# Waiting on PE instead of SP for the last store of a two-branch decode attention

## The chip, the cores and the metric

The kernel runs on one core of one Trainium2 chip. A core has five engines with an instruction stream of their own: PE (TensorE, the matrix multiplier), DVE (VectorE), ACT (ScalarE), POOL (GpSimd) and SP (SyncE, which here only issues transfers). They meet through semaphores alone. The metric is the device time of one execution in microseconds (us). Three runs of the kernel before gave 246.31, 246.37 and 246.56 us; their median, 246.37 us, is the time before.

## The reference

Two independent decode attentions, A and B, are computed for one token each and their results laid side by side. Both have a row x of 576 numbers, 32 query heads on 16 key and value heads, heads of 128, and caches of 8192 positions; all is bf16.

```
def _B_ref(x, k_cache, v_cache, wq, wo):
    q = (x @ wq).reshape(B, Sq, Hq, Dh).transpose(0, 2, 1, 3)
    k = jnp.repeat(k_cache, rep, axis=1)          # rep = 2
    v = jnp.repeat(v_cache, rep, axis=1)
    scores = jnp.einsum("bhqd,bhkd->bhqk", q, k) * (Dh ** -0.5)
    p = _softmax(scores, axis=-1)
    o = jnp.einsum("bhqk,bhkd->bhqd", p, v)
    return o.transpose(0, 2, 1, 3).reshape(B, Sq, Hq * Dh) @ wo
```

A is the same on the last W = 2048 positions of its caches. The result is [1, 1, 1152]: 576 numbers of A, then 576 of B.

## The kernel before

The kernel is a list of operations for each engine, written by hand: `op(eng, fn, deps, name)` appends an operation to one engine's list, `load(...)` appends one that increments a semaphore of its own when it is done (a transfer counts 16). When all is listed, `emit` walks each list in order and writes the engine's instructions. In front of an operation it writes a wait (line 83, `eng.wait_ge(s, v)`) for each semaphore value that the operation needs and that this engine has not yet waited for. An operation whose function is `None` is its waits and nothing else. Every wait made by the kernel therefore stands under line 83 in the profile, unless it was joined to the instruction behind it. Nothing reorders the lists.

The work runs in this order. SP issues all large loads into one ring in SBUF: the query weights of A and B, then the keys and values of eight units (four of A, four of B, each of four key heads), then the output weights. The output weights of A are one load; those of B come in five pieces of 17, 8, 4, 2 and 1 blocks (`NWO`), so that little work is left when the last piece has landed. PE makes the queries (line 310). For each unit DVE transposes the keys in slabs (line 350), PE makes the scores (line 367), a softmax without its division follows on DVE, PE and ACT, DVE transposes the probabilities (lines 414 and 418) and PE multiplies with the values (line 431). The sums of the exponentials are divided out at the end (lines 488 to 499).

The last stage is the output projection (line 510): for each of A and B, 64 matmuls with one column of weights each into two rows of one PSUM bank. When a branch's last matmul is done, ACT copies 320 of its numbers and DVE the other 256 to the row `outsb` (lines 519 and 521), each adds 1 to that branch's semaphore `s_row`, and SP issues the store of 1152 bytes (line 523), which adds 16 to `s_out` when it has landed. The store of A is named `out0` and that of B `out1`; `out1` stands for `s_out` at 32, which both stores make up. The last operation of the kernel is a wait for `out1` with no function.

POOL writes constants at the start and has nothing to do after that. ACT and DVE have nothing behind their copies of B's output, PE nothing behind its last matmul of line 510.

Of the kernel before, what the change touches and what calls it, by code (L numbers as in the profile page):

```python
# [36 lines left out]
class Prog:  # L37
# [9 lines left out]
    def op(self, eng, fn, deps=(), name=None):  # L47
        self.ops[eng].append((fn, tuple(deps), name, None))
        if name is not None:
            assert name not in self.where, name  # L50
            self.where[name] = (eng, len(self.ops[eng]) - 1)
# [46 lines left out]
def bass_concat_heads__sliding_block_cached__gqa_block_cached__decode_kernel(nc, A_x, A_k_cache, A_v_cache, A_wq, A_wo,  # L98
# [59 lines left out]
    op, load = pg.op, pg.load  # L158
# [74 lines left out]
    def slab(kind, i, s):  # L233
# [10 lines left out]
       deps=["id0"], name="ident")  # L244
# [15 lines left out]
    for c in range(2):  # L260
        op("dve", lambda e, c=c: e.tensor_reduce(par[:, c:c + 1], view(identf, 128, c, [[2, 64]]), AX.X, ALU.add),
           deps=["identf"], name="par%d" % c)
# [3 lines left out]
    for P in range(2):  # L266
# [14 lines left out]
        for c in range(2):  # L281
            op("dve", lambda e, P=P, c=c: e.tensor_scalar(
                xrep[:, P, 4 + c, :], banks[2 * P + 1][:, 0:128], par[:, c:c + 1], None, ALU.mult),
                deps=["xT%d.4" % P, "par%d" % c], name="xr%d.%d" % (P, 1 + c))
# [3 lines left out]
       deps=["identf"], name="clsb")  # L288
    op("dve", lambda e: e.tensor_reduce(clsa[:], view(identf, 128, 0, [[1, 8], [8, 16]]), AX.X, ALU.add),
       deps=["identf"], name="clsa")  # L290
    op("dve", lambda e: e.tensor_reduce(sel[:], view(identf, 128, 0, [[1, 32], [32, 4]]), AX.X, ALU.add),
       deps=["identf"], name="sel")
# [6 lines left out]
    for P in range(2):  # L299
        for n in range(8):  # L300
# [3 lines left out]
            def mm(e, P=P, n=n, bank=bank):  # L304
# [10 lines left out]
               deps=["qmm%d.%d" % (P, n)] + (["qT%d" % (u // 2 - 2)] if u >= 4 else []), name="qe%d" % u)  # L315
            if n % 2:
# [3 lines left out]
                    deps=["qe%d" % (u - 1), "qe%d" % u] + (["z0.%d" % i for i in range(4)] if P else []),  # L320
                    name="qT%d" % (u // 2))
        for b in range(4):
            if P == 1:
# [3 lines left out]
                    deps=["qT%d" % u for u in range(4, 8)] + ["zb0"], name="z1.%d" % b)  # L327
            else:
# [3 lines left out]
                    deps=["qT%d" % u for u in range(4)] + ["za0"], name="z0.%d" % b)  # L332
# [122 lines left out]
    for i in range(NU):  # L455
# [34 lines left out]
       deps=["lsel", "lselA", "nb%d" % last, "mr%d" % last], name="L")  # L490
# [3 lines left out]
        deps=["rl", "O%d" % last], name="on")  # L494
    op("dve", lambda e: e.transpose(oq[:].rearrange("p c k -> p (c k)"), on[:].rearrange("p c k -> p (c k)")),
       deps=["on"], name="oq")
# [6 lines left out]
    for P in range(2):  # L503
        k0 = 0
        for c, kk in enumerate(NWO[P]):
            def mm(e, P=P, c=c, k0=k0, kk=kk):
# [15 lines left out]
             s_row[P], 2, deps=[done], step=1)  # L522
        load("sp", lambda e, lo=lo: e.dma_start(out[0, 0:1, lo:lo + DM], outsb[0:1, lo:lo + DM]),
             s_out, 16 * (P + 1), deps=["f%d" % P], name="out%d" % P)
    op("sp", None, deps=["out1"])

    pg.emit()

# [27 lines left out]
```

## Time and profile before

| what | value |
|---|---|
| median of three runs | 246.37 us (246.31 to 246.56) |
| the profiled execution's own time | 246.6 us |
| its span, first to last instruction | 245.2 us |
| busy: PE, DVE, ACT, POOL | 172.3, 129.1, 24.3, 8.2 us |
| moved by the transfers | 102.90 MB, mean 420 GB/s |
| the last copies of the output row, on ACT and DVE, start | 243.65 us |
| each of these two copies takes | 0.43 us |
| issue of the last store, until SP's last wait is over | 244.1 to 245.2 us |

The page of the profile gives for each engine its busy time and share of the span, a picture of the span in 40 slices, the transfer queues, the chain of work that ended last, and the costliest groups of instructions. The timeline, the chain and the waits come from the same trace. Times count from the span's start. An engine's name with a q behind it (SPq, PEldq) is its sequencer, which waits and issues; such instructions are not counted as busy. The span ends with the last instruction of the program; the profiled execution's own time is 1.4 us longer.

### The profile page before, as it was taken

The page shows a single profiled execution, that of the slowest core. Times are in us where ns is not written, and L with a number is a line of the kernel's source. Part 1 is how long each engine was busy: PE and PEld are TensorE (multiplying, and loading weights), DVE is VectorE, ACT ScalarE, POOL GpSimd, SP SyncE. Part 2 cuts the span into 40 slices and gives each one's busy share as a digit, 9 for nine tenths or more (in the row PEclk, how much of TensorE's full clock was granted, in tenths as well). Part 3 has the DMA queues.
Part 4 walks back from the last instruction along what each step waited for, and adds up shares of the span by engine and source line. Part 5 has one row for each costly group of instructions (what it writes and reads, how often), then busy time and mean ns, then how long its engine had stood idle before and what let it go on. Part 6 is the DMA issues. An engine that isn't in the chain of part 4 may idle for free.

```text
span 245.2 us, 2253 instructions
## 1 busy us (share of the span) xinstructions
PE 172.3 (70%) x960; PEld 71.8 (29%) x961; DVE 129.1 (53%) x162; ACT 24.3 (10%) x52; POOL 8.2 (3%) x15
## 2 busy tenths in 40 slices
PE   0269967787867994889582869945579939257197
PEld 0124422224433222432130523211423213213154
DVE  0422547667789986699501699810679920500201
ACT  2004540021201000100000100000010000200001
POOL 8400000000000000000000000000000000000000
PEclk9999995789999997569957578989657985677559
DMA  7999999999999999998999999999999999999994
GB/s 267 420 457 410 437 428 425 433 428 457 440 430 387 468 428 428 452 470 385 406 428 425 438 476 428 438 406 425 438 466 460 395 406 430 428 438 409 430 407 158
DMA packets 4481, 102.90 MB, mean 420 GB/s; under 512 B 500, under 2 KB 632, under 8 KB 1144
## 3 DMA queue, kind: packets, MB, share of 16 engines
q1 hardware_dynamic: 4468, 102.76, 97.9%
q8 instruction: 7, 0.11, 0.2%
q14 instruction: 2, 0.02, 0.0%
q10 hardware_dynamic: 4, 0.00, 0.0%
HBM read 102.76 MB, written 0.00 MB: 419 GB/s over the span
## 4 chain that ended last, share of the span: by engine, by line
DMA 55%; PE 29%; DVE 12%; ACT 2%; issue 2%; SPq 0%; DVEq 0%
DMA ring<-in_B_v_cache_dram 40%; DMA ring<-in_A_wo_dram 10%; DVE ktb L350 9%; PE vb L431 8%; DMA ring<-in_A_wq_dram 5%; PE qb L367 5%; PE qb L510 5%; PE sb L310 5%; PE qb L310 4%; ACT psb L406 1%; DVE pta L414 1%; PE ob L447 1%; PE sb L367 1%; PE qb L359 1%; PE mb L397 1%
## 5 line engine op out<-in xcount | busy, mean ns | idle before, releaser
L350 DVE STREAM_TRANSPOSE ktb<-ring 128x1024 int32<-128x1024 int32 x80 | 92.8, 1211 | 29.5 <-DMA ring<-in_B_k_cache_dram 28.3
L367 PE MATMUL sb<-ktb,zb 128*128 128x512 bf16 x256 | 76.0, 437 | 23.7 <-DVE ktb L350 21.1
L367 PEld LDWEIGHTS sb<-ktb,zb 128*128 128x128 bf16 x256 | 23.4, 106 | 72.4 <-DVE ktb L350 45.9
L431 PE MATMUL vb<-ring,pts 128*32 128x512 bf16 x256 | 24.7, 567 | 18.5 <-DMA ring<-in_B_v_cache_dram 14.4
L367 PE MATMUL qb<-ktb,za 128*128 128x512 bf16 x64 | 19.4, 449 | 2.8 <-DVE ktb L350 2.8
L431 PEld LDWEIGHTS vb<-ring,pts 128*32 128x32 bf16 x256 | 9.0, 134 | 33.6 <-DMA ring<-in_B_v_cache_dram 16.7
L438 ACT ACTIVATE xo<-vb 128x512 f32<-128x512 f32 x8 | 4.8, 597 | 129.4 <-PE vb L431 129.4
L418 DVE STREAM_TRANSPOSE pts<-psb 32x512 bf16<-32x512 bf16 x16 | 11.3, 703 | 9.5 <-ACT psb L406 9.3
L510 PE MATMUL qb<-ring,oP 128*1 128x256 bf16 (+1 forms) x128 | 11.3, 340 | 4.0 <-DMA ring<-in_A_wo_dram 4.0
L317 DVE STREAM_TRANSPOSE ktb<-qsb 128x512 int32<-128x512 int32 x8 | 5.7, 711 | 15.0 <-ACT qsb L314 15.0
L310 PE MATMUL sb<-ring,xrep 128*128 128x512 bf16 x40 | 11.4, 442 | 2.7 <-DMA ring<-in_A_wq_dram 2.7
L447 PEld LDWEIGHTS ob<-sel,xo 128*128 128x128 f32 x64 | 10.9, 244 | 3.8 <-ACT xo L438 2.2
L447 PE MATMUL ob<-sel,xo 128*128 128x8 f32 x64 | 10.1, 285 | 1.2 <-ACT xo L438 1.2
L367 PEld LDWEIGHTS qb<-ktb,za 128*128 128x128 bf16 x64 | 6.1, 109 | 13.4 <-issue 5.8
L310 PE MATMUL qb<-ring,xrep 128*128 128x512 bf16 x39 | 9.5, 393 | 0.0
L510 PEld LDWEIGHTS qb<-ring,oP 128*1 128x1 bf16 x128 | 7.0, 93 | 8.3 <-DMA ring<-in_A_wo_dram 4.1
L521 DVE CAST outsb<-qb 1x256 bf16<-1x256 f32 x2 | 0.8, 420 | 14.7 <-PE qb L510 14.7
L491 DVE RECIPROCAL rl<-mb 128x64 f32<-128x64 f32 x1 | 0.6, 558 | 12.3 <-PE mb L488 12.3
L276 PE MATMUL sb<-onesb,xrow 1*128 1x128 bf16 x4 | 0.6, 298 | 9.2 <-DVE xdup L267 9.2
L392 DVE TENSOR_REDUCE mr<-mb 1x8 f32<-1x128 f32 x8 | 1.9, 240 | 9.5 <-PE mb L384 9.5
L310 PEld LDWEIGHTS sb<-ring,xrep 128*128 128x128 bf16 x40 | 4.3, 109 | 8.6 <-issue 5.3
L314 ACT ACTIVATE qsb<-sb 128x512 bf16<-128x512 f32 x8 | 4.8, 597 | 19.1 <-PE sb L310 19.1
(65 smaller groups left out, 68.8 us busy)
## 6 DMA issues: line engine op xcount, KB each, us to landing
ring<-in_B_k_cache_dram SPq DMA_DIRECT2D x8, 4096.0 KB, 24.5
ring<-in_A_k_cache_dram SPq DMA_DIRECT2D x4, 2048.0 KB, 30.5
ring<-in_A_v_cache_dram SPq DMA_DIRECT2D x4, 2048.0 KB, 25.4
ring<-in_B_v_cache_dram SPq DMA_DIRECT2D x2, 4096.0 KB, 23.8
ring<-in_A_wo_dram SPq DMA_DIRECT2D x1, 4608.0 KB, 23.9
ring<-in_A_wq_dram SPq DMA_DIRECT2D x1, 4096.0 KB, 12.5
ring<-in_B_wq_dram SPq DMA_DIRECT2D x1, 4096.0 KB, 22.6
ring<-in_B_wo_dram SPq DMA_DIRECT2D x1, 2448.0 KB, 29.3
```

Of the source, the lines that this page charges most:

```text
L310: ins = e.matmul(bank[:, :], lhsT=lhsT, rhs=o, start=(k == 0), stop=(k == 4))
L314: op("act", lambda e, u=u, bank=bank: e.activation(qsb[:, u % 4, :], bank[:, :], ACT.Copy), deps=["qmm%d.%d" % (P, n)] + (["qT%d" % (u // ...
L317: op("dve", lambda e, u=u, n=n: e.transpose(ktb[:, (n - 1) * 512:(n + 1) * 512].bitcast(I32), qsb[:, u % 4 - 1:u % 4 + 1, :].rearrange("p ...
L350: op("dve", lambda e: e.transpose(kt.bitcast(I32), src.bitcast(I32)), deps=[landed] + (["S%d" % (k - NKT)] if k >= NKT else Z), name="T%d. ...
L359: e.matmul(bank[:, :], lhsT=mkl[:].rearrange("p a h r -> p (a h r)"), rhs=mkr[:].rearrange("p q h -> p (q h)"), start=True, stop=False)
L367: ins = e.matmul(bank[:, :], lhsT=lhsT, rhs=view(ktb, KT, (k % NKT) * SLAB + 64 * c + v, [[128, 16], [2, 32]]), start=(side == "B" and s = ...
L397: op("pe", lambda e: e.matmul(mb[:, 128:129], lhsT=mexp[0:1, :], rhs=onesf[0:1, 0:1], start=True, stop=True), deps=["mx%d" % i, "ones"], n ...
L418: op("dve", lambda e, b=b: e.transpose(view(pts, NB * 128, 2 * b, [[8, 16], [128, NB], [1, 2]], 32, 32 * b), psb[32 * b:32 * b + 32, :]), ...
L431: ins = e.matmul(vbank[i][32 * j:32 * j + 32, :], lhsT=lhsT, rhs=src[:, 512 * j:512 * j + 512], start=(s == 0), stop=(s == nslab[i] - 1))
L438: op("act", lambda e: e.activation(xo[:, c, :], vbank[i][:, :], ACT.Copy), deps=["V%d.%d" % (i, nslab[i] - 1)] + (["O%d" % (i - 1)] if i e ...
L447: ins = e.matmul(ob[:, at:at + 8], lhsT=xo[:, c, 128 * t:128 * t + 128], rhs=sel[:, 8 * t:8 * t + 8], start=(t == 0), stop=(t == 3))
L510: ins = e.matmul(fb[r:r + 1, 0:hi - lo], lhsT=oP[:, P, k0 + k:k0 + k + 1], rhs=wo_at[P, c][:, k * DM + lo:k * DM + hi], start=(k0 + k == 0 ...
```

## The change

The last operation, the wait for the last store, is put into PE's list; SP's list then ends with the issue of that store. In the built programs SP has one instruction less and PE one more, its last: a wait for `s_out` to reach 32. All other instructions, their order and their waits are the same.

```
         load("sp", lambda e, lo=lo: e.dma_start(out[0, 0:1, lo:lo + DM], outsb[0:1, lo:lo + DM]),
              s_out, 16 * (P + 1), deps=["f%d" % P], name="out%d" % P)
-    op("sp", None, deps=["out1"])
+    op("pe", None, deps=["out1"])
 
     pg.emit()
```

## The prediction

> **What bounds the kernel now.** I read the page first: span, transfers, and the chain that ended last.
>
> ```profile
> span 245.2 us, 2253 instructions
> DMA  7999999999999999998999999999999999999994
> DMA 55%; PE 29%; DVE 12%; ACT 2%; issue 2%; SPq 0%; DVEq 0%
> ```
>
> The transfers are busy from the second slice to the last but one: the loads bound the kernel, and the change touches none of them. So only the end matters. I read it in the chain of work (its last three pieces) and in the timeline of the last microseconds.
>
> ```profile
> 232.32 11.31 PE qb L510 x94
> 243.63 0.02 issue
> 243.65 0.43 ACT outsb L519
> ```
>
> ```profile
> 240.20 4.15 SPq L523 DMA_DIRECT2D out_dram<-outsb  x2
> 243.65 0.43 ACT L519 ACTIVATE outsb<-qb 1x320 bf16<-1x320 f32 x1 [3.47 <-PE qb L510]
> 243.65 0.43 DVE L521 CAST outsb<-qb 1x256 bf16<-1x256 f32 x1 [3.49 <-PE qb L510]
> ```
>
> PE's last matmul ends at 243.6, the copies at 244.08; SP issues the second store at 244.11 and is free of it at 244.35 (the timeline's row merges both issues). Then nothing runs but the store. The waits of SP's queue and the rows of line 83 show the wait that is moved, and what such a wait costs on either engine:
>
> ```profile
> SPq L83 <- DMA out_dram<-outsb: 0.9, 1, 0.9
> ```
>
> ```profile
> L83 PEldq EVENT_SEMAPHORE  x18: 51/51/2202, 9.0 to 228.6; - x18
> L83 SPq EVENT_SEMAPHORE  x5: 17/17/17, 54.4 to 245.2; - x5
> ```
>
> The reader should see that the last 0.9 us is one wait for a landing which no choice of the waiting engine makes earlier, and that the instruction takes 17 ns on SP and 51 ns on PE (the 2202 ns is a wait for two semaphores at 23.4 us, at the start of the queries). So what counts is what follows the landing.
>
> **What follows the landing.** The profiled execution's own time is 246.6 us against a span of 245.25, so 1.35 us lie outside, and they need an explanation, since the moved wait stands right before them. No view lists them, but the trace also records every change of a semaphore, beyond the last instruction too. I read these events there, in us from the span's start:
>
> - 245.216: the last store's semaphore is complete. SP's wait starts at 245.233 and ends at 245.250.
> - One semaphore (number 2), which the kernel does not use, changes nine times: 243.790; 244.196, 244.234, 244.279; 245.366; 245.410, 245.449, 245.483, 245.531.
> - From 245.494 to 246.126 the other semaphores are cleared, in five groups of about 50 numbers; the group 7 to 53 starts last (245.781) and ends last (246.126).
> - Semaphore 2 changes nine times again, 246.350 to 246.706, and the execution's time falls into this stretch.
>
> I read the nine changes as a round of the five engines, up and back: each adds one when it has come to its end and the one before it has added, the fifth turns round, and four are passed on the way back. The times say who stands where. The first change, 243.790, follows PE's last matmul (its semaphore: 243.629) by 0.161; no other engine ends near that time, so the head of the round is PE. The second follows the ends of ACT and DVE (244.08) by 0.11. The fifth follows SP's wait by 0.116 and waited for it alone, so SP is the turning point. The way back thus ends at PE, and the engine that is released last also clears last. These places are inferred from the times; no row names the engine.
>
> **The change part by part.**
>
> Removed: on SP, a wait of 17 ns that starts 17 ns after the landing; from the landing to SP's step in the round 0.150 us. SP is free at 244.35 and then stands in the round waiting for the others. Nothing is queued behind it that could run sooner: no transfer follows the store.
>
> Added: on PE, a wait of 51 ns. It takes the start of two weight loads of line 510 that waited for the last two pieces of B's output weights: 42 ns and 41 ns after the landings (a third: 72). From the wait's end to PE's step I take SP's 0.116; the upper bound is the 0.161 that PE needed after its last matmul. So from landing to step: 0.042 + 0.051 + 0.116 = 0.209, bounds 0.150 (as SP's) and 0.072 + 0.051 + 0.161 = 0.284. Against SP's 0.150 that is +0.06, bounds 0 and +0.13. Behind the waiting PE there is no matmul, only its end and the round; the other four engines now wait for PE in that round, as they waited for SP before.
>
> Moved: the place in the round from which the rest runs. Before, four changes lay ahead of the landing, hidden by the store (0.9 us), and after SP's step only the way back remained: 245.531 − 245.366 = 0.165. With PE last, the whole round runs after the landing. Its price is shown by the two rounds that nothing delays: 0.356 (246.350 to 246.706) and, ahead of the kernel, 0.371 (from −0.370 to 0.001). So +0.191 to +0.206; I take +0.20. The lower bound is eight steps at the pace of the way back, 8 × 0.041 = 0.33, or +0.165. A gain is not excluded by the rows if I have the places wrong: with PE at the turning point and SP at the head, the 0.20 would change its sign, and the sum would be 0.06 − 0.20 = −0.14.
>
> The clearing and the second round come after PE's release in both kernels and keep their length (245.531 to 246.706), so they shift as a whole. The store, its issue and all before it cost nothing either way: the same instructions in the same order up to 244.35, and the cover named above, the 0.9 us of the store, is the part that PE's step in the round loses.
>
> Sum: 0.06 + 0.20 = +0.26 us, bounds +0.165 and +0.34. Against the profiled execution: 246.6 + 0.26 = 246.9. That execution stands 0.2 above the median of the runs, so on the median 246.37 + 0.26 = 246.63 us, or 0.11%. A measurement of this kernel tells about 0.2%, 0.49 us, from no change (its three runs spread over 0.25). The shift is real by my reading, and under that.
>
> The Trainium skill (Runtime: NRT & Kernel Launch, section on the preamble and postamble breakdown) has an end barrier of about 1.5 us in its table, in which all engines are awaited. By that figure, were all of it pushed behind the landing, the estimate would be 246.37 + 1.5 = 247.9 us. The trace does not agree: the undelayed rounds took 0.356 and 0.371. The same section gives 355 ns for the bare pass over five engines, in 8 hops of 44 ns; four hops more would be +0.18 instead of my +0.20.
>
> **The rivals.**
>
> *No difference.* The order of the round is not as I read it, or the time is read at a point that the shift does not reach. Then only the dearer wait remains, 0 to +0.13, or −0.14 with the places exchanged: 246.4 us (246.23 to 246.50). For it: no row names an engine in the round. Against it: the change at 243.790 fits PE alone.
>
> *Clearly slower: a block of instructions that isn't there.* PE's instructions are fetched while it runs: the page counts seven transfers of kind "instruction" on queue q8 (0.11 MB), each taking 1.02 to 1.10 us in the trace, the last at 236.06. Between their starts PE's recorded instructions number 220 to 288, 260 on average; from the last fetch to PE's end there are 189, so the next boundary lies some 70 on, among what PE does at its end. One more instruction there, and a standing PE in front of it, could lay a fetch open: 246.63 + 1.08 = 247.7. It decides if the block that PE needs after its wait is not yet in. Against it: no block was waited for in the clearing of the last group now (two numbers in a row stand 4 to 11 ns apart, to the end), and the last fetch was over 8 us before the end.
>
> *Faster.* SP, which issued all transfers, is freed 0.9 us earlier. If SP's end, and not PE's, carried the time, and went ahead during the store, up to 0.9 us would go: 245.5. It decides if the time is taken at SP's end and SP passes without waiting for PE. Against it: SP's step came fifth, after four others, and the clearing starts only after it.
>
> *The wait does nothing.* PE would pass with 16 of 32 counted, or the wait be dropped. It stands last in PE's list, for both stores' 32, so I leave it out.
>
> **How the numbers follow.** My forecast, +0.165 to +0.34, 246.53 to 246.71: 0.64, of which 0.03 for a measurement that scatters beyond 246.86. No difference: 0.17. Clearly slower: 0.15. Faster: 0.04. So faster by over 0.2% 0.04; within 0.2% 0.61 + 0.17 = 0.78; slower by over 0.2% 0.15 + 0.03 = 0.18. The time is the forecast's, 246.63. The range holds the forecast and no difference, and above 246.71 the runs' own spread of 0.25: 246.2 to 246.95; what it leaves out are the last two rivals, 0.19.
>
> **What the changed profile would show.** Row L83 of SPq has 4 instructions and none at 245.2; that of PEldq has 19, the last near 245.25 after the span's start, 51 ns long, so that the span grows by about 0.06. SP's queue no longer waits for out_dram. In the semaphore events, none of the nine changes lies ahead of the landing: the first comes some 0.2 us after it and the other eight within 0.37, the group 7 to 53 still ends last, about 0.25 later after the landing than now. If four changes still lie ahead of the landing, my order of the engines is wrong, and the time should be unchanged. If a gap of about 1 us stands behind PE's wait, or an eighth block on q8 in it, the fetch was open. If the second round begins earlier after the landing than 246.350 − 245.216 = 1.134, the change gained, and my reading of the end is wrong.

## The result and the profile after

With the wait on PE the kernel takes 246.63 us (median of 22 runs, 246.43 to 246.85) against 246.33 us before (22 runs, 246.16 to 246.56). The ratio is 1.0013 with a 95% interval of 1.0007 to 1.0018: 0.30 us longer. The interval lies clear of no change, and the change is less than 0.2%.

The page of the changed kernel, its span, its transfers and the chain that ended last:

```profile
span 245.1 us, 2254 instructions
...
DMA  7999999999999999998999999989999999999994
...
DMA 55%; PE 29%; DVE 12%; ACT 2%; issue 2%; SPq 0%; DVEq 0%
```

The span is no longer than before (245.1 against 245.2 in the two profiled executions): nearly all of what became longer must lie outside it. The end of the chain, in order of time, and the timeline of the last microseconds:

```profile
232.11 11.29 PE qb L510 x94
243.40 0.02 issue
243.43 0.43 ACT outsb L519
```

```profile
240.05 4.08 SPq L523 DMA_DIRECT2D out_dram<-outsb  x2
...
243.43 0.42 DVE L521 CAST outsb<-qb 1x256 bf16<-1x256 f32 x1 [3.41 <-PE qb L510]
243.43 0.43 ACT L519 ACTIVATE outsb<-qb 1x320 bf16<-1x320 f32 x1 [3.40 <-PE qb L510]
```

All is in its old order, 0.2 us earlier because this execution's loads were a little faster (PE starts its last piece of the chain at 232.11 us, before at 232.32). Two rows show the moved wait, line 83 of the changed kernel (duration in ns: least, median, longest; then first and last start in us):

```profile
L83 PEldq EVENT_SEMAPHORE  x19: 51/51/2119, 9.0 to 245.0; - x19
...
L83 SPq EVENT_SEMAPHORE  x4: 17/17/17, 54.3 to 92.6; - x4
```

PE now has a nineteenth wait, at 245.0, and SP no longer has its fifth. In the waits of SP's queue the row for out_dram is gone; its first row now:

```profile
SPq L217 <- DVE ktb L350: 87.5, 7, 19.6
```

The rest is in the changes of semaphore 2, which the trace records and no view lists. A round is nine such changes in a row. Times in us from the span's start, for the profiled execution of each kernel:

| | before | with the change |
|---|---|---|
| second store has landed | 245.216 | 244.988 |
| the wait, start to end | 245.233 to 245.250 | 245.016 to 245.067 |
| first round, the nine changes | 243.790; 244.196, 244.234, 244.279; 245.366; 245.410, 245.449, 245.483, 245.531 | 245.259, 245.294, 245.332, 245.376, 245.400, 245.497, 245.537, 245.574, 245.620 |
| group 7 to 53 is cleared | 245.781 to 246.126 | 245.833 to 246.180 |
| second round, first and last change | 246.350, 246.706 | 246.405, 246.764 |

Before, four changes lie ahead of the landing and five behind. With the change all nine lie behind it. From the landing to the end of the wait it is 0.034 us before and 0.079 with the change, so the wait itself lengthens the span by only 0.045 us. From the landing to the end of the second round it is 1.490 us before and 1.776 with the change: +0.286, which is the 0.30 of the medians to within the scatter of this stretch.

A measure that scatters less than the time helps below: the time less the span, run by run. The span holds the loads and scatters with them. What is left lies ahead of the first instruction or behind the last one, and the wait for the store is not in it. It was 1.59 us on average in the 22 runs of the change, and 1.32 to 1.34 in three sets of 21 to 28 runs of the kernel before that the experiments brought. Its standard deviation within a set is at most 0.04.

### The profile page after: what moved, and what is told of

Its sections match the earlier page's. It is cut to its first block, busy times and chain, and to the rows that moved or that the text cites. A ratio compares the mean times of both kernels' runs of the same rounds, so it can differ in the third digit from the quotient of the medians.

```text
span 245.1 us, 2254 instructions
## 1 busy us (share of the span) xinstructions
PE 171.8 (70%) x961; PEld 71.3 (29%) x961; DVE 129.0 (53%) x162; ACT 24.3 (10%) x52; POOL 8.1 (3%) x15
## 4 chain that ended last, share of the span: by engine, by line
DMA 55%; PE 29%; DVE 12%; ACT 2%; issue 2%; SPq 0%; DVEq 0%
DMA ring<-in_B_v_cache_dram 40%; DMA ring<-in_A_wo_dram 10%; DVE ktb L350 9%; PE vb L431 8%; DMA ring<-in_A_wq_dram 5%; PE qb L367 5%; PE qb L510 5%; PE sb L310 4%; PE qb L310 4%; ACT psb L406 1%; DVE pta L414 1%; PE ob L447 1%; PE sb L367 1%; PE qb L359 1%; PE mb L397 1%
## 5 line engine op out<-in xcount | busy, mean ns | idle before, releaser
L367 PE MATMUL sb<-ktb,zb 128*128 128x512 bf16 x256 | 75.2, 430 | 23.9 <-DVE ktb L350 20.8
L367 PEld LDWEIGHTS sb<-ktb,zb 128*128 128x128 bf16 x256 | 22.7, 105 | 72.5 <-DVE ktb L350 48.0
L510 PE MATMUL qb<-ring,oP 128*1 128x320 bf16 (+1 forms) x128 | 11.3, 341 | 4.0 <-DMA ring<-in_A_wo_dram 4.0
```

The costliest lines, as they stand in the source:

```text
L367: ins = e.matmul(bank[:, :], lhsT=lhsT, rhs=view(ktb, KT, (k % NKT) * SLAB + 64 * c + v, [[128, 16], [2, 32]]), start=(side == "B" and s = ...
L510: ins = e.matmul(fb[r:r + 1, 0:hi - lo], lhsT=oP[:, P, k0 + k:k0 + k + 1], rhs=wo_at[P, c][:, k * DM + lo:k * DM + hi], start=(k0 + k == 0 ...
```

## The experiments

The theory is that each engine has a place in a round, PE the first and SP the last before the turn. An engine's step is the change of semaphore 2 that it makes on the way up; the way back from the turn follows. The steps behind the place of the engine that waits are what the store no longer hides. The rivals are that the cost is PE's own (its 51 ns and a slow end), that an instruction more at PE's end costs, or that the loss comes from SP no longer waiting. Every kernel below is the one before with the edit shown.

**The wait on ACT, DVE and POOL.**

```
-    op("sp", None, deps=["out1"])
+    op("act", None, deps=["out1"])      # or "dve", or "pool"
```

> The wait for the last store stands on ACT. Theory of the place in the round: ACT follows PE, so after the landing come its step, three steps up and four back. From the undelayed round of before (steps at 0, 0.034, 0.073, 0.116, 0.139, 0.237, 0.275, 0.309, 0.356 us) that is 0.356 - 0.034 = 0.32 us behind ACT's step against 0.165 behind SP's: +0.16 us, and up to +0.1 for the wait itself; 246.33 + 0.16 to 0.26 = 246.5 to 246.6. One change of semaphore 2 (PE's) lies ahead of the landing, eight after it. Rival, that the cost is PE's own (its 51 ns wait and its slow end): ACT's wait took 17 ns as SP's did, so 246.3 to 246.4. Rival, that only SP may wait cheaply: as PE, 246.63.

> The wait stands on DVE. Theory of the place: DVE is third or fourth in the round; the trace shows it by two or three changes of semaphore 2 ahead of the landing. Behind its step 0.356 - 0.073 = 0.28 us (third) or 0.356 - 0.116 = 0.24 us (fourth), against 0.165: +0.12 or +0.08 us, and up to +0.1 for the wait; 246.4 to 246.55. Rival, that the cost is PE's own: 246.3 to 246.4. Rival, that only SP may wait cheaply: 246.63.

> The wait stands on POOL. Theory of the place: POOL has the place that DVE does not have, third or fourth, with two or three changes of semaphore 2 ahead of the landing: +0.12 or +0.08 us, and up to +0.1 for the wait; 246.4 to 246.55. Rival, that the cost is PE's own: 246.3 to 246.4. Rival, that only SP may wait cheaply: 246.63.

Measured, against 246.29 us before: ACT 246.47 (ratio 1.0009, 1.0000 to 1.0018), DVE 246.60 (1.0014, 1.0004 to 1.0023), POOL 246.97 (1.0030, 1.0018 to 1.0041). The rows of line 83 show the wait in its place, 17 ns on ACT (first row, from the kernel with the wait on ACT) and on POOL (second row, from the kernel with it there), 21 ns on DVE (third row, likewise):

```profile
L83 ACTq EVENT_SEMAPHORE  x14: 17/17/17, 20.9 to 245.0; - x14
```

```profile
L83 POOLq EVENT_SEMAPHORE  x1: 17/17/17, 245.1 to 245.1; - x1
```

```profile
L83 DVEq EVENT_SEMAPHORE  x18: 21/21/21, 9.8 to 244.9; - x18
```

The semaphore events place all five engines. With the wait on ACT one change lies ahead of the landing, on POOL two, on DVE three, on SP four, on PE none. So the round goes PE, ACT, POOL, DVE, SP and back. In us, from the profiled executions:

| wait on | place | landing to its step | its step to the end of round 1 | to the end of round 2 | sum | more than SP |
|---|---|---|---|---|---|---|
| SP (before) | 5 | 0.150 | 0.165 | 1.175 | 1.490 | |
| DVE | 4 | 0.195 | 0.241 | 1.146 | 1.582 | 0.09 |
| POOL | 3 | 0.583 | 0.285 | 1.149 | 2.017 | 0.53 |
| ACT | 2 | 0.152 | 0.323 | 1.149 | 1.624 | 0.13 |
| PE (the change) | 1 | 0.271 | 0.361 | 1.144 | 1.776 | 0.29 |

The sums of the four other kernels in which SP waited for the landing last lie between 1.46 and 1.50, against 1.490 for the one in the table, so the last column is good to a few hundredths. The fourth column falls by the place as the theory said: 0.32, 0.28 and 0.24 were worked out for places 2, 3 and 4, and 0.323, 0.285 and 0.241 came. That the cost is PE's own is refuted by ACT, whose wait takes 17 ns as SP's does and whose step follows the landing just as soon (0.152 against 0.150): in the events it still costs 0.13 us, all of it behind its step. In the medians the gain of SP over ACT (0.18 us) is only at the edge of its interval; the time less the span has it plainly, 1.47 against 1.34. ACT's time lies just under its expected range, which was counted from 246.33; the difference to its own base, 0.18 us, lies in the 0.16 to 0.26 expected.

Two numbers did not fit. POOL takes its step 0.583 us after the landing where up to 0.25 was allowed, so its time missed the expected 246.4 to 246.55. And DVE's time, 246.60, is above its expected range: the events give 0.09 us more than SP, the medians 0.31. Counted from the span's start, the profiled execution's time ends 0.10 to 0.11 us ahead of the second round's last change in every kernel so far but this one, in which it ends 0.105 us behind it (246.59 against 246.485). The time less the span is 1.65 in the mean of eleven runs, so it was no single run. Both were taken up below.

**One wait more on PE, met long before.**

```
+    op("pe", None, deps=["f0"])
     op("sp", None, deps=["out1"])
```

> SP keeps the wait for the last store; PE gets one instruction more at its end, a wait for the copies of A's output, which were done some 3 us earlier. Theory of the place: PE takes its step about 0.05 to 0.1 us later than before, still over 1 us ahead of the landing, and the time is that of before, 246.33 (246.25 to 246.4). Rival, that an instruction more at PE's end costs by itself (its 51 ns, a block of instructions): 246.6 as with the change, or more.

Measured: 246.27 us against 246.29 (ratio 0.9998, 0.9989 to 1.0007), time less span 1.33. The changes are at 243.495; 243.904, 243.942, 243.986; 245.069 and so on, the landing at 244.919: the old order. PE's step follows its last matmul's semaphore by 0.157 us, before by 0.161, so the delay of 0.05 to 0.1 us that was expected did not come: the added wait starts at 243.016 us, under PE's last matmuls, which end at 243.316. Met there, one instruction more on PE costs nothing that shows, and no fetch of a block of instructions was laid open. What 51 ns cost where nothing covers them, this run does not tell.

**SP and PE both wait.**

```
+    op("pe", None, deps=["out1"])
     op("sp", None, deps=["out1"])
```

> SP and PE both wait for the last store. Theory of the place: PE, at the head, sets the end; SP's wait is over long before the round reaches it. The time is that of the change, 246.6 (246.5 to 246.75), and all nine changes of semaphore 2 come after the landing. Rival, that the loss comes from SP no longer waiting (SP's end work done early and in the way of the store): with SP's wait back the time is that of before, 246.33.

Measured: 246.58 us against 246.35 (1.0010, 1.0001 to 1.0019), time less span 1.58. SP's wait is back, as its queue shows for this kernel:

```profile
SPq L83 <- DMA out_dram<-outsb: 0.9, 1, 0.9
```

All nine changes come behind the landing (244.911), the first 0.271 us after it as with the change alone. So the loss does not come from SP no longer waiting; it is PE's lateness in the round.

**PE late by work instead of by a wait.** Four or ten matmuls whose product nobody reads are added behind PE's last one; SP waits as before.

```
+    def tailmm(e):
+        for _ in range(4):              # or 10
+            ins = e.matmul(vb[0][:, :], lhsT=zb[:, 0, 0, 0:128], rhs=ktb[:, 0:512], start=True, stop=True)
+        return ins
+    op("pe", tailmm, name="tail")
     op("sp", None, deps=["out1"])
```

> SP waits as before; behind its last matmul of the output projection PE makes four matmuls more of 512 columns into a bank that is done with. At 0.136 us per 320 columns (the pace of those matmuls) that is 4 x 0.218 = 0.87 us. Theory of the place: PE's step moves from 243.79 to about 244.7 us, the landing is at 245.2, the store still covers the head of the round: 246.33 (246.25 to 246.4). Rival, that PE's end is in the time by itself: up to +0.87, 247.2.

> As the run with four matmuls, with ten: 2.18 us. Theory of the place: PE's step moves to 243.79 + 2.18 = 245.97, past the landing and SP's wait; all nine changes of semaphore 2 follow it, the way back ends at 245.97 + 0.36 = 246.33 against 245.53 before: +0.80 us, 247.1 (247.0 to 247.3). Rival, that a late engine costs its lateness and an end like SP's (0.116 + 0.165 us) whatever its place: PE's last matmul ends at 243.63 + 2.18 = 245.81, the round at 246.09: +0.56, 246.9.

Measured, against 246.35: four matmuls 246.41 us (1.0004, 0.9995 to 1.0013), ten 247.17 us (1.0035, 1.0022 to 1.0047), or +0.82. The timelines of the kernel with four and of that with ten have the added work (line 527):

```profile
243.34 1.04 PE L527 MATMUL vb<-ktb,zb 128*128 128x512 bf16 x4
```

```profile
243.39 2.33 PE L527 MATMUL vb<-ktb,zb 128*128 128x512 bf16 x10
```

With four, PE's step comes at 244.528, still 0.485 us ahead of the landing (245.013), and 1 us of matmuls costs nothing that shows: the time less the span is 1.32 us in both kernels. With ten it comes at 245.869, behind the landing (245.063) and SP's wait, and the whole round follows it: 0.359 us, as where PE waits. The rival in which the place does not count gave +0.56 and falls; +0.80 was expected.

**DVE's 0.21 us.** Two kernels: once with SP waiting and a wait on DVE that is met long before, once with DVE waiting and one of its early instructions given to POOL.

```
+    op("dve", None, deps=["f0"])
     op("sp", None, deps=["out1"])
```

> With the wait on DVE the time was 0.21 us longer than its semaphore events give: the time less the span was 1.65 us, and 1.43 were expected from the end of the second round. Here SP keeps the wait for the last store, and DVE has one instruction more, a wait for something met long before. If it is the instruction more (DVE has 182 instead of 181) that costs the 0.21 us, wherever the last wait stands, the time less the span is 1.33 + 0.21 = 1.54 us and the time 246.5. If it belongs to a wait of DVE that is the last to be met, they are 1.33 and 246.3.

```
-    op("dve", lambda e: e.tensor_scalar(mkl[:], ...), deps=["ident"], name="mkl")
+    op("pool", lambda e: e.tensor_scalar(mkl[:], ...), deps=["ident"], name="mkl")
...
-    op("sp", None, deps=["out1"])
+    op("dve", None, deps=["out1"])
```

> DVE waits for the last store, and one instruction of its early work (the mask mkl, line 293) is done on POOL, so that DVE has 181 instructions as before. If the 0.21 us came from the number of instructions, the time less the span is 1.43 us and the time 246.33 + 0.12 = 246.45. If it belongs to a wait of DVE that is the last to be met, they are 1.65 and 246.6.

Measured, against 246.30: the added wait 246.48 us (1.0009, 1.0000 to 1.0018), time less span 1.55; DVE waiting with 181 instructions 246.40 us (1.0005, 0.9996 to 1.0014), time less span 1.43 (the kernel before, measured beside them: 1.32). Both are the numbers expected if the count of DVE's instructions costs the 0.21 us, and neither fits the other reading. With 181 instructions the wait on DVE costs 0.12 us by the time less the span, about what its place and its wait come to in the table (0.09). The median alone would not have told this: the second kernel's interval, −0.10 to +0.34 us, holds both readings. The semaphore events say the same: the second kernel repeats the stretches of the first kernel with the wait on DVE (0.195, 0.241 and 1.145 us), and only the time is shorter. In all twelve kernels here the time goes by this count: in the ten with 181 instructions on DVE it ends 0.10 to 0.11 us ahead of the second round's last change, in the two with 182 it ends 0.105 and 0.114 us behind it.

Why the 182nd instruction on DVE costs 0.2 us while one more on PE costs nothing stays open. The trace shows no event in that stretch, and it does not show where the device time begins and ends, so the 0.2 us may lie at either end. That it is the count, and not something else that these two kernels share, is argued from the pattern; the mask on POOL was not tried by itself.

**POOL's 0.58 us.**

```
+    op("pool", None, deps=["f1"])
     op("sp", None, deps=["out1"])
```

> With the wait on POOL its step came 0.54 us after the wait's end, where the other engines took 0.12 to 0.19. Here SP keeps the wait for the last store, and POOL waits for the copies of B's output (met at about 244.1 us). If the 0.54 us are what POOL takes from its last wait to its step, the third change of semaphore 2 comes 0.54 us after the end of POOL's wait, at about 244.65, still ahead of SP's step, and the time is that of before, 246.3. If they belong to the wait for a store, POOL's step comes 0.12 to 0.2 us after its wait; the time is 246.3 too.

Measured: 246.27 us against 246.30 (0.9999, 0.9991 to 1.0008). POOL's wait ends at 243.849 us by the trace and the third change comes at 244.391, 0.542 us later; with the wait for the store it was 0.543 (245.068 to 245.611). So POOL takes 0.54 us from its last wait to its step for both of the things it waited for; the store's landing hides it in this kernel and exposes it where POOL waits for the landing.

## Why the prediction was right

The time was forecast at 246.63 us and is 246.63; the bound of 0.2% was not reached; that the shift is there all the same was forecast too. That the time agrees to the hundredth is luck: the larger set of runs puts the kernel before at 246.33, 0.04 under the 246.37 that was taken, and the shift is +0.30, 0.04 over the +0.26 that was forecast. What was right is the mechanism and a shift inside its bounds, +0.165 to +0.34. By its steps:

- *The bound and the cover.* Right. Loads, output projection and store are as they were, and the 0.9 us of the store covered the head of the round before. The runs with four and ten added matmuls show that cover directly: 1 us of added work on PE is free, 2.3 us are not.
- *Who stands where in the round.* It was inferred from the times of one trace, PE first and SP fifth. The five places of the wait show it: none, one, two, three or four changes ahead of the landing.
- *The moved place*, +0.20 us forecast. It is 0.361 − 0.165 = +0.196 by the two traces.
- *The dearer wait*, +0.06 forecast with bounds 0 and +0.13. It is 0.271 − 0.150 = +0.12: right in sign, but twice the forecast, and near the upper bound. The term that was too small is the time from the wait's end to PE's step. SP's 0.116 was taken for it, with 0.161 as the upper bound; it measured 0.192, and 0.191 in the kernel in which SP and PE both wait. The start after the landing (0.028, 0.042 taken) made up a little. The 0.161 that PE needed after its last matmul was the nearer neighbour, and even it was too low; why PE needs longer after a wait, no run shows.
- *What follows PE's release*, forecast to keep its length. It was 1.175 us before and 1.144 with the change. The four other kernels where SP met the landing last gave 1.150, 1.146, 1.150 and 1.181, so 0.03 is what this stretch scatters. In that one pair of profiles it hid part of the dearer wait: 0.196 + 0.121 − 0.031 = 0.286.
- *The signs named in the profile.* The rows of line 83 and of SP's queue and the nine changes behind the landing are as described, and the group 7 to 53 still ends last, 0.28 us later after the landing than before (about 0.25 forecast). The second round begins 1.417 us after the landing, not under the 1.134 that would have meant a gain. That the span grows by 0.06 can't be seen in the span of one profile, since the loads scatter by more; from the landing to the end of the wait it is +0.045.
- *The estimate from the Trainium skill.* The Trainium skill (Runtime: NRT & Kernel Launch, preamble and postamble breakdown) has about 1.5 us for an end barrier in which all engines are awaited. That much did not come behind the landing: the whole round took 0.361 us there. Whether the page's figure also holds time in which engines wait for one another, no run here shows.
- *The rivals.* No difference: excluded by the interval, which in us is +0.17 to +0.44, against 0 to +0.13 for the dearer wait alone. A block of instructions that isn't there: there is no gap of 1 us behind PE's wait, and the page still counts seven such transfers on q8. Faster because SP is free: the kernel became slower, and with SP's wait put back beside PE's the time stayed at 246.58.

```profile
q8 instruction: 7, 0.11, 0.2%
```

No kernel was faster than the one before beyond its interval. By the table the wait belongs where it stood: SP has the fewest steps behind it and as short a way to its step as any.

## What to carry to other kernels

The end of a program can be part of its measured time. Here the engine that is late there sets it, and which engine waits for the last store decides how much of the end the store still hides. In this kernel the wait belongs on the engine at the turn of the round (SP), and the engine at its head (PE) should be free early. Work at PE's end is free up to its slack: 1 us of it cost nothing. Beyond the slack it counts nearly in full: with ten matmuls PE's step came 0.535 us later after the landing than with the wait on PE (0.806 against 0.271), and the loss grew from 0.30 to 0.82 us. Whether another program has the same order of engines must be read from its own trace.

The whole effect of the change is a few tenths of a microsecond. So read it in the events of the trace and in the time less the span; the medians alone hardly separate such cases.

## What was not expected of the hardware

- POOL needs 0.54 us from its last wait to its step in the round, ACT and SP 0.11 to 0.12, DVE 0.15, PE 0.19. It is the dearest of the five to wait on in this kernel, 0.68 us over the kernel before in the medians, though it had nothing else to do.
- One more instruction on DVE, met at once and 1.5 us ahead of the landing, made the time less the span 1.55 us instead of 1.32, with the same span. The cause is not known, and one more on PE (1.33 us) or on POOL (1.32 us) did not show it.
